# Attention and a gated FFN in one kernel: the first batch's loads laid out and queued anew

## The chip, the cores and the metric

One core of a Trainium2 chip. The metric is device microseconds of one execution. A profile of one execution comes with it; its times are counted from the start of the profiled span.

## The reference

Inputs q, k, v are (batch 8, heads 8, sequence 576, head width 64) in float32. The FFN has model width 512 and inner width 1536.

```python
kv  = einsum('bhsd,bhse->bhde', k, v)
out = einsum('bhsd,bhde->bhse', q, kv)
out = out / sqrt(mean(out*out, -1) + 1e-6) * g_norm
x   = out.transpose(0, 2, 1, 3).reshape(4608, 512)
xn  = x / sqrt(mean(x*x, -1) + 1e-6) * rms_g
y   = (silu(xn @ w_gate) * (xn @ w_val)) @ w_out
```

There is no softmax, so k and v are first reduced to one 64x64 matrix per head, and q is multiplied with that. A sum over tokens may be taken in any grouping of them, provided that k and v are grouped alike.

## The kernel before

The 576 tokens of a batch are cut into 512 "main" tokens and 64 of "remainder". The main tokens lie on 128 partitions with four consecutive tokens each (`NC = 4` chunks), the remainder on 64 partitions with one token each, as a fifth chunk whose other 64 partitions hold zeros. Heads go in four pairs (`j` from 0 to 3), two heads side by side in one 128x128 matmul; `P0` is pairs 0 and 1, `P1` pairs 2 and 3. `H0` and `H1` are the first and last four heads. After the attention of a batch its 512 main tokens go through the FFN, the remainders of all eight batches together at the end. Matmuls are in bf16.

The order of instructions on each engine is written by hand (later batches by a planner with fixed costs, `Placer`). Only the first batch (`Att(0)`) matters here, and of it the first half, chunks 0 and 1 of q, on which the FFN's first matmuls depend:

- Loads: v by POOL's queue with a cast to bf16 on the way (remainder, `H0`, `H1`), straight to `vc[0]`. k by SP's queue as float32 (`H0`, remainder, `H1`). q's chunks 0 and 1 by ACT's queue, then the gains (`grow`, three small loads). q's chunks 2 and 3 are issued on SP and ACT by a wait that is added by hand, once `v_loads[0]`, v's remainder, has landed. The weights follow v on POOL's queue.
- PE: 18 idle matmuls (`spin`, L232), the transposes of q (`qT_mm`, L298), a transpose of the gains (L798), four more idle matmuls, then the kv products of `P0` (`kv_pairs`, L279), o for the statistics (`oT_mm`, L368), the kv products of `P1`, and so on through the statistics (L393), o (L340), the transposes of x (L509) to the first gate matmuls (L662). An engine runs its instructions in the order in which they stand.
- DVE: the memsets at the start (L158 to L169; `idle` among them, which the first spin reads), casts of q's half, of k's `H0` and of k's remainder, the copy of qT of `P1`, the gains, then the masked copies of kv (L286).
- ACT: the copy of qT of `P0` (L320), the cast of k's `H1` (L203), the squares (L379).
- POOL, behind the weights' loads: memsets, and the casts of q's rest (L203, L210).

`kv_pairs` and `pair` take every chunk of a pair:

```python
for c in self.kv_chunks:                 # NC + 1 of them
    nc.tensor.matmul(ps[:, i, :], lhsT=self.pair(1, c, j), rhs=self.pair(2, c, j), ...)
```

Of the kernel before, what the change touches and what calls it, by code (L numbers as in the profile page):

```python
# [10 lines left out]
FP32 = mybir.dt.float32  # L11
BF16 = mybir.dt.bfloat16
# [74 lines left out]
def kernel(  # L87
# [12 lines left out]
    nc = tc.nc  # L100
    B, H, S, D = q.shape
# [3 lines left out]
    NC = 4  # L105
    MAIN = 128 * NC
    REM = S - MAIN
# [9 lines left out]
    pool = lambda name, bufs, **kw: ctx.enter_context(tc.tile_pool(name=name, bufs=bufs, **kw))  # L117
    consts = pool("consts", 1)
    stage = pool("stage", 3)
    rstage = pool("rstage", 4)  # L120
    qkv = pool("qkv", 2)
    outa_p = pool("outa", 6)
    sq_p = pool("sq", 3)
# [17 lines left out]
    vc, kc = ([consts.tile([128, H, (NC + 1) * D], BF16, name=f"{t}c{n}") for n in range(2)] for t in "vk")  # L141
    sel = consts.tile([128, 2, 2], BF16, name="sel")
    qc = consts.tile([128, H, (NC + 1) * D], BF16, name="qc1")
# [8 lines left out]
    wo = [consts.tile([128, OB, d_model], BF16, name=f"wo{n}") for n in range(NF // OB)]  # L152
    kvs = [consts.tile([128, NS, 2, D], BF16, name=f"kvs{n}") for n in range(2)]
    qTs = [consts.tile([128, NC + 1, NS, 128], BF16, name=f"qTs{n}") for n in range(2)]
    rems = [[consts.tile([128, H, D], BF16, name=f"rem{t}{n}") for n in range(m)] for t, m in (("q", 2), ("k", 1))]
    xr = consts.tile([128, NS, MAIN], BF16, name="xr")
    for t in range(2):
        nc.vector.memset(rems[t][0][REM:], 0.0)  # L158
    nc.vector.memset(vc[0][REM:, :, NC * D :], 0.0)
    idle = consts.tile([128, MAIN], BF16, name="idle")  # L160
    nc.vector.memset(idle, 0.0)  # L161
    nc.vector.memset(diag, 0.0)
# [9 lines left out]
    src = (q, k, v)  # L172
# [3 lines left out]
    def load_main(b, t, heads=(0, H), cs=(0, NC), queue=nc.sync):  # L176
        if (b, t) not in staged:
            staged[b, t] = stage.tile([128, H, NC * D], FP32, name="stg")
        h0, h1 = heads
        view = src[t][b, :, 0:MAIN, :].rearrange("h (p c) d -> p h (c d)", c=NC)  # L180
        return queue.dma_start(
            out=staged[b, t][:, h0:h1, cs[0] * D : cs[1] * D], in_=view[:, h0:h1, cs[0] * D : cs[1] * D]
        )

    def load_cast(b, t, heads=None):
        to = qc if t == 0 else (vc if t == 2 else kc)[b % 2]
        if heads is None:
            return nc.gpsimd.dma_start(
                out=to[:REM, :, NC * D :], in_=src[t][b, :, MAIN:S, :].rearrange("h p d -> p h d")
            )  # L190
        view = src[t][b, :, 0:MAIN, :].rearrange("h (p c) d -> p h (c d)", c=NC)[:, heads[0] : heads[1]]
        return nc.gpsimd.dma_start(out=to[:, heads[0] : heads[1], : NC * D], in_=view)

    def load_rem(b, t, queue=nc.sync):
        rstaged[b, t] = rstage.tile([REM, H, D], FP32, name="rstg")
        return queue.dma_start(out=rstaged[b, t], in_=src[t][b, :, MAIN:S, :].rearrange("h p d -> p h d"))

    def cast_main(b, t, eng, heads=(0, H), cs=(0, NC)):
        if (b, t) not in mains:
            mains[b, t] = qkv.tile([128, NC, H, D], BF16, name=f"main_{'qkv'[t]}")  # L200
        h0, h1 = heads
        copy = eng.copy if eng is nc.scalar else eng.tensor_copy
        return copy(  # L203
            out=mains[b, t][:, cs[0] : cs[1], h0:h1, :],
            in_=staged[b, t].rearrange("p h (c d) -> p c h d", c=NC)[:, cs[0] : cs[1], h0:h1, :],
        )

    def cast_rem(b, t, eng):
        copy = eng.copy if eng is nc.scalar else eng.tensor_copy
        copy(out=rems[t][b % 2][:REM], in_=rstaged[b, t])  # L210
# [6 lines left out]
    def loads_kv(b):  # L217
        return [lambda t=t, hs=hs: load_cast(b, t, hs) for t in (1, 2) for hs in ((0, H), None)]
# [11 lines left out]
    def spin(ps, n):  # L230
        for _ in range(n):
            nc.tensor.matmul(ps, lhsT=idle[:, :128], rhs=idle, start=True, stop=True, skip_group_check=True)  # L232

    def flat(ps):
        return ps.rearrange("p j t -> p (j t)")

    class Att:
# [35 lines left out]
        def kv_pairs(self, js, wait=0):  # L273
            ps = mm1_p.tile([128, 4, 2 * D], FP32, name="mm1")
            spin(flat(ps), wait)
            ps = ps[:, : len(js)]
            for i, j in enumerate(js):
                for c in self.kv_chunks:
                    nc.tensor.matmul(  # L279
                        ps[:, i, :], lhsT=self.pair(1, c, j), rhs=self.pair(2, c, j),  # L280
                        start=i == 0 and c == 0, stop=i == len(js) - 1 and c == NC, skip_group_check=True,
                    )
            return ps

# [472 lines left out]
    V, G, A = nc.vector, nc.gpsimd, nc.scalar  # L757
    H0, H1 = (0, 4), (4, 8)
    P0, P1 = (0, 1), (2, 3)
    ALL = range(NS)  # L760
    v_loads = [load_cast(0, 2, hsx) for hsx in (None, H0, H1)]
    load_main(0, 1, H0)
    load_main(0, 0, cs=(0, 2), queue=A)
    load_rem(0, 1)
    load_main(0, 1, H1)
    A.preload_act_table(ACT.Sqrt)
    A.dma_start(out=grow[0:NS], in_=moe_rms_g.rearrange("(s p) -> s p", p=128))
    for half in range(2):
# [9 lines left out]
    w_loads = [load_w(n) for n in range(len(FB))]  # L778
    G.memset(rems[0][1][REM:], 0.0)
    G.memset(kvs[1], 0.0)  # L780
    for tile_ in (kc[0], kc[1], vc[1], qc):
        G.memset(tile_[REM:, :, NC * D :], 0.0)

    def fold(w, s, eng):
        if eng == "ACT":
            A.mul(out=w[:, s], in_=w[:, s], mul=gain[:, s : s + 1])  # L786
        else:
            V.tensor_scalar(out=w[:, s], in0=w[:, s], scalar1=gain[:, s : s + 1], scalar2=None, op0=OP.mult)

    spin(mm1_p.tile([128, MAIN], FP32, name="mm1"), 18)  # L790
    a = Att(0)
    cast_main(0, 0, V, cs=(0, 2))
    cast_main(0, 1, V, H0)
    cast_rem(0, 1, V)
    for js, eng in ((P0, A), (P1, V)):
        a.qT_out(a.qT_mm(js, (0, 1)), js, 0, eng)
    gT = o2_p.tile([128, NS + 1], FP32, name="o2")
# [3 lines left out]
    for half in range(2):  # L801
        rows = slice(half * D, (half + 1) * D)
        V.tensor_tensor(out=sel[rows, 1, half : half + 1], in0=gcol[rows], in1=gcol[rows], op=OP.mult)
    V.tensor_scalar(
        out=gain, in0=gall[:, 0:NS], scalar1=gcol, scalar2=float(d_model) ** 0.5, op0=OP.mult, op1=OP.mult
    )
    kva = a.kv_pairs(P0, 4)
    cast_main(0, 1, A, H1)
    for i, j in enumerate(P0):
        a.kv_pairs_out(kva, i, j)  # L810
    ta = a.oT_mm(P0, 0, 2, o2_p, 2)
# [23 lines left out]
    for t in (0, 2, 1):  # L835
        load_cast(1, t, (0, H))
        load_cast(1, t)
# [6 lines left out]
    for n, w in enumerate(FB):  # L844
        js = range(FB0[n], FB0[n] + w)
# [68 lines left out]
    for b in range(1, B):  # L914
# [9 lines left out]
        if b == 1:  # L924
            for n, at in ((0, 6), (1, 24), (2, 30), (3, 40)):
                for j in range(NS):
                    for w, eng, cost in ((wg, "DVE", 0.09), (wv, "ACT", 0.13)):
                        f = P.put(eng, cost * FB[n], lambda w=w, n=n, j=j, e=eng: fold(w[n], j, e), at=starts[1] + at + j)
# [36 lines left out]
```

## Time and profile before

| | us |
|---|---|
| median of 3 runs | 329.57 (329.0 to 476.69) |
| the profiled execution, its own time | 329.4 |
| its span | 327.6 |
| PE busy | 318.6 (97% of the span) |
| DVE, ACT, POOL busy | 176.0, 144.5, 89.0 |
| PE busy in 0 to 10 / 10 to 20 / 20 to 40 us | 7.50 / 7.52 / 20.00 |
| first kv product (L279) | 11.44 |
| first gate matmul (L662) | 18.55 |

The execution takes 1.8 us more than its span, for what lies before the first and after the last instruction. Busy time on PE counts the idle matmuls too. In the timelines a row gives start, duration, engine, source line, operation, output and inputs, count, and in brackets how long the engine had been idle and what ended that.

### The profile page before, as it was taken

What the parts mean: (1) busy time and instruction counts of PE and PEld (TensorE: products, weight loads), DVE (VectorE), ACT (ScalarE), POOL (GpSimd) and SP (SyncE); (2) the same over time, 40 slices, a digit from 0 to 9 for tenths busy, and PEclk for the clock granted to TensorE, in tenths of its full rate; (3) what the DMA queues carried; (4) which work ended last, traced back from release to release, by engine and by line L of the source; (5) the groups of instructions that cost most, each with busy time, mean ns of one, the idle gap of its engine ahead of it and who ended that gap; (6) DMA issues with size and microseconds to landing.
All of it is one profiled execution on the core that took longest, in us unless ns stands there. A gap on an engine that the chain in (4) does not pass through costs nothing.

```text
span 327.6 us, 5425 instructions
## 1 busy us (share of the span) xinstructions
PE 318.6 (97%) x2060; PEld 162.2 (49%) x2060; DVE 176.0 (54%) x392; ACT 144.5 (44%) x269; POOL 89.0 (27%) x109
## 2 busy tenths in 40 slices
PE   7789999999999999999999999999999999999995
PEld 2468765554445444544454445444544444444443
DVE  3458446679928681768077807781687234203411
ACT  1375446776658422842274227421752233223320
POOL 8663320028205800580058004900420000000000
PEclk9999999999999999999999999999999999999999
DMA  8999999774994895589557966696000800020013
GB/s 193 227 200 199 194 223 212 179 175 53 167 208 136 103 157 161 145 98 140 161 167 84 136 166 176 70 148 168 35 1 0 170 32 0 13 116 2 0 34 96
DMA packets 78741, 40.49 MB, mean 124 GB/s; under 512 B 42744, under 2 KB 74236, under 8 KB 78716
## 3 DMA queue, kind: packets, MB, share of 16 engines
q0 software_dynamic: 30928, 14.16, 34.2%
q1 hardware_dynamic: 46048, 25.08, 31.9%
q10 hardware_dynamic: 1740, 0.92, 1.0%
q8 instruction: 16, 0.26, 0.3%
q14 instruction: 9, 0.07, 0.1%
HBM read 37.78 MB, written 9.44 MB: 144 GB/s over the span
## 4 chain that ended last, share of the span: by engine, by line
PE 94%; DMA 3%; DVE 1%; issue 0%; POOL 0%; ACT 0%; DVEq 0%; POOLq 0%
PE mm L634 57%; PE o L669 26%; DMA vc<-in_v_dram 3%; PE att L331 2%; PE att L268 2%; PE mm L669 2%; PE o L698 1%; PE att L309 1%; PE o L368 0%; DVE xna L350 0%; PE att L509 0%; PE mm L279 0%; PE att L368 0%; PE mm L662 0%; PE mm L232 0%
## 5 line engine op out<-in xcount | busy, mean ns | idle before, releaser
L652 DVE TENSOR_TENSOR h<-silu,mm 128x512 bf16<-128x512 bf16 (+1 forms) x120 | 75.7, 632 | 79.6 <-PE mm L634 69.3
L643 ACT ACTIVATE silu<-mm 128x512 bf16<-128x512 f32 (+1 forms) x120 | 66.4, 556 | 89.1 <-PE mm L634 80.2
L634 PE MATMUL mm<-x,wv 128*128 128x512 bf16 (+1 forms) x432 | 99.8, 355 | 0.0
L634 PE MATMUL mm<-x,wg 128*128 128x512 bf16 (+1 forms) x420 | 98.7, 358 | 0.0
L669 PE MATMUL o<-wo,h 128*128 128x512 bf16 x396 | 89.9, 379 | 0.0
L414 POOL TENSOR_TENSOR sq<-sq,g 128x512 bf16<-128x512 bf16 x30 | 34.4, 1153 | 134.2 <-ACT sq L357 134.2
L634 PEld LDWEIGHTS <-wg 128*128 128x128 bf16 x468 | 45.0, 98 | 45.9
L634 PEld LDWEIGHTS <-wv 128*128 128x128 bf16 x480 | 45.4, 98 | 40.9
L669 PEld LDWEIGHTS <-h 128*128 128x128 bf16 x420 | 40.3, 98 | 46.9
L685 ACT COPY osb<-o 128x512 f32<-128x512 f32 x33 | 19.3, 589 | 67.8 <-PE o L669 67.8
L419 DVE TENSOR_REDUCE st<-sq 128x8 f32<-128x512 bf16 x60 | 38.4, 679 | 0.0
L292 DVE CAST kvs<-att 64x256 bf16<-64x256 f32 x14 | 5.9, 422 | 39.5 <-PE att L268 39.4
L483 DVE TENSOR_TENSOR xna<-outa,al 128x512 bf16<-128x512 bf16 x35 | 21.8, 686 | 0.0
L357 ACT ACTIVATE sq<-att 128x512 bf16<-128x512 f32 x30 | 18.2, 607 | 0.0
L361 ACT CAST outa<-att 128x512 bf16<-128x512 f32 x30 | 17.8, 594 | 0.0
L331 PEld LDWEIGHTS <-qTs 128*128 128x128 bf16 x140 | 9.8, 98 | 5.2
L634 PE MATMUL mm<-xr,wg 128*128 128x512 bf16 x48 | 12.3, 379 | 0.0
L634 PE MATMUL mm<-xr,wv 128*128 128x512 bf16 x48 | 12.3, 379 | 0.0
L331 PE MATMUL att<-kvs,qTs 128*128 128x128 bf16 x140 | 11.7, 219 | 0.0
L203 POOL CAST main_q<-stg 128x1024 bf16<-128x1024 f32 (+1 forms) x12 | 11.4, 987 | 0.1
L232 PE MATMUL mm<-idle 128*128 128x512 bf16 x27 | 8.0, 455 | 2.1 <-DVE idle L161 2.1
L786 ACT ACTIVATE wv<-wv,gain 128x384 bf16<-128x384 bf16 x16 | 9.2, 612 | 0.2 <-PE mm L634 0.2
(130 smaller groups left out, 175.4 us busy)
## 6 DMA issues: line engine op xcount, KB each, us to landing
out_dram<-osb SPq DMA_DIRECT2D x32, 256.0 KB, 2.3
stg<-in_q_dram SPq DMA_DIRECT2D x6, 1024.0 KB, 6.8
vc<-in_v_dram POOLq DMA_DIRECT2D x7, 512.0 KB, 8.4
kc<-in_k_dram POOLq DMA_DIRECT2D x7, 512.0 KB, 6.2
wg<-in_moe_w_gate_dram POOLq DMA_DIRECT2D x4, 384.0 KB, 16.1
wv<-in_moe_w_val_dram POOLq DMA_DIRECT2D x4, 384.0 KB, 17.1
wo<-in_moe_w_out_dram POOLq DMA_DIRECT2D x4, 384.0 KB, 13.6
stg<-in_k_dram SPq DMA_DIRECT2D x2, 512.0 KB, 7.1
```

Of the source, the lines that this page charges most:

```text
L203: return copy(out=mains[b, t][:, cs[0] : cs[1], h0:h1, :], in_=staged[b, t].rearrange("p h (c d) -> p c h d", c=NC)[:, cs[0] : cs[1], h0:h ...
L331: nc.tensor.matmul(o[:, 2 * j : 2 * j + 2, :], lhsT=self.qTj[:, j, c, :], rhs=self.kv[:, j, :, :], start=j == 0, stop=j == NS - 1, skip_gr ...
L357: nc.scalar.activation(out=self.sq[c][:, 0], in_=self.o[c], func=ACT.Square)
L361: (eng.tensor_copy if eng else nc.scalar.copy)(out=self.outa[c], in_=self.o[c])
L414: eng.tensor_tensor(out=self.sq[c][:, 1], in0=self.sq[c][:, 0], in1=g2, op=OP.mult)
L419: nc.vector.reduce_sum(out=self.st[:, which, c, :], in_=self.sq[c][:, which], axis=AX.X)
L483: return eng.tensor_tensor(out=self.xna[:, c], in0=src, in1=self.al[:, c, :].to_broadcast([128, H, D]), op=OP.mult)
L634: nc.tensor.matmul(ps[:, : c1 - c0], lhsT=w[n][:, s, jj * 128 : (jj + 1) * 128], rhs=x_of(g, s, c0, c1), start=s == 0, stop=s == NS - 1)
L643: nc.scalar.activation(out=sis[g, j][:, c0:c1], in_=ps, func=ACT.Silu)
L652: nc.vector.tensor_tensor(out=hs[g, j][:, c0:c1], in0=sis[g, j][:, c0:c1], in1=v_ps, op=OP.mult)
L669: nc.tensor.matmul(ps, lhsT=hs[g, j][:, t * 128 : (t + 1) * 128], rhs=wo[j // OB][:, j % OB, :], start=j == 0, stop=j == NF - 1)
L685: (eng.copy if eng is nc.scalar else eng.tensor_copy)(out=o, in_=ps)
```

## The change

- v's and k's remainders of the first batch are laid out as 32 partitions of two consecutive tokens each: `vr` and `krT`, new tiles. A packet of the load is then 512 B and not 256 B, and there are 256 of them and not 512.
- The kv sum of the first batch has six chunks: four main and two of remainder. Each pair has six matmuls.
- The two new tiles are cleared below row 32 by four DVE memsets; the old ones for k's remainder and `vc[0]` go. `vc[0]`, which a later batch still uses, is cleared on POOL.
- k's `H0` stays on SP's queue, k's `H1` goes from SP's to ACT's as its first load, q's half goes from ACT's to SP's behind k's `H0`. k's remainder goes from SP's to ACT's queue, behind k's `H1`, into a buffer of the pool `stage`; the pool `rstage` has two buffers and not four.
- On DVE the cast of k's `H0` stands before that of q's half, and the cast of k's remainder (32x1024) after it. On ACT the cast of k's `H1` stands before the copy of qT. In the program as built, ACT's third gains load waits until k's `H1` has landed.

```diff
-    rstage = pool("rstage", 4)
+    rstage = pool("rstage", 2)
...
-    rems = [[... name=f"rem{t}{n}") for n in range(m)] for t, m in (("q", 2), ("k", 1))]
+    rems = [[consts.tile([128, H, D], BF16, name=f"remq{n}") for n in range(2)]]
+    krT = consts.tile([128, 2, H, D], BF16, name="remk")
+    vr = consts.tile([128, H, 2, D], BF16, name="remv")
...
-    for t in range(2):
-        nc.vector.memset(rems[t][0][REM:], 0.0)
-    nc.vector.memset(vc[0][REM:, :, NC * D :], 0.0)
+    for tile_, rows in ((krT, REM // 2), (vr, REM // 2), (rems[0][0], REM)):
+        for r0 in (rows, 2 * rows) if rows < REM else (rows,):
+            nc.vector.memset(tile_[r0 : REM if r0 < REM else 128], 0.0)
...
+    def two(t):
+        return src[t][0, :, MAIN:S, :].rearrange("h (p c) d -> p h (c d)", c=2)
...
-                for c in self.kv_chunks:
+                for c in range(NC + 2):
+                    h = slice(2 * j, 2 * j + 2)
+                    if c < NC:
+                        k_, v_ = self.pair(1, c, j), self.pair(2, c, j)
+                    else:
+                        k_, v_ = krT[:, c - NC, h, :], vr[:, h, c - NC, :]
...
-    v_loads = [load_cast(0, 2, hsx) for hsx in (None, H0, H1)]
+    v_loads = [G.dma_start(out=vr[: REM // 2].rearrange("p h c d -> p h (c d)"), in_=two(2))]
+    v_loads += [load_cast(0, 2, hsx) for hsx in (H0, H1)]
     load_main(0, 1, H0)
-    load_main(0, 0, cs=(0, 2), queue=A)
-    load_rem(0, 1)
-    load_main(0, 1, H1)
+    load_main(0, 1, H1, queue=A)
+    load_main(0, 0, cs=(0, 2))
+    krst = stage.tile([128, H, NC * D], FP32, name="stg")[: REM // 2, :, : 2 * D]
+    A.dma_start(out=krst, in_=two(1))
...
-    for tile_ in (kc[0], kc[1], vc[1], qc):
+    for tile_ in (kc[0], kc[1], vc[0], vc[1], qc):
...
+    cast_main(0, 1, V, H0)
+    cast_main(0, 1, A, H1)
     cast_main(0, 0, V, cs=(0, 2))
-    cast_main(0, 1, V, H0)
-    cast_rem(0, 1, V)
+    V.tensor_copy(out=krT[: REM // 2], in_=krst.rearrange("p h (c d) -> p c h d", c=2))
...
     kva = a.kv_pairs(P0, 4)
-    cast_main(0, 1, A, H1)
```

More of the change, by code (lines that the diff above doesn't have):

```diff
@@ L154 @@
     qTs = [consts.tile([128, NC + 1, NS, 128], BF16, name=f"qTs{n}") for n in range(2)]
-    rems = [[consts.tile([128, H, D], BF16, name=f"rem{t}{n}") for n in range(m)] for t, m in (("q", 2), ("k", 1))]
+    rems = [[consts.tile([128, H, D], BF16, name=f"remq{n}") for n in range(2)]]
+    krT = consts.tile([128, 2, H, D], BF16, name="remk")
+    vr = consts.tile([128, H, 2, D], BF16, name="remv")
     xr = consts.tile([128, NS, MAIN], BF16, name="xr")
-    for t in range(2):
-        nc.vector.memset(rems[t][0][REM:], 0.0)
-    nc.vector.memset(vc[0][REM:, :, NC * D :], 0.0)
+    for tile_, rows in ((krT, REM // 2), (vr, REM // 2), (rems[0][0], REM)):
+        for r0 in (rows, 2 * rows) if rows < REM else (rows,):
+            nc.vector.memset(tile_[r0 : REM if r0 < REM else 128], 0.0)
     idle = consts.tile([128, MAIN], BF16, name="idle")
@@ L277, in kv_pairs @@
             for i, j in enumerate(js):
-                for c in self.kv_chunks:
+                for c in range(NC + 2):
[4 more added lines that the diff above has]
+                        k_, v_ = krT[:, c - NC, h, :], vr[:, h, c - NC, :]
                     nc.tensor.matmul(
-                        ps[:, i, :], lhsT=self.pair(1, c, j), rhs=self.pair(2, c, j),
-                        start=i == 0 and c == 0, stop=i == len(js) - 1 and c == NC, skip_group_check=True,
+                        ps[:, i, :], lhsT=k_, rhs=v_,
+                        start=i == 0 and c == 0, stop=i == len(js) - 1 and c == NC + 1, skip_group_check=True,
                     )
```

## The prediction

> **What bounds the kernel now.** I read the page first. The chain that ended last is PE work almost throughout, with one DMA left on it.
>
> ```profile
> PE 94%; DMA 3%; DVE 1%; issue 0%; POOL 0%; ACT 0%; DVEq 0%; POOLq 0%
> ```
>
> From about 18.5 us on PE runs without a hole worth naming, so the end moves only if the start of that stream moves. What sets the start is in the chain in order of time, cut to the first 20 us (start, us, what):
>
> ```profile
> 1.26 0.86 POOL vc L188
> 2.12 9.27 DMA vc<-in_v_dram
> 11.40 0.04 issue
> 11.44 0.72 PE mm L279 x10
> ```
>
> The first kv products (L279) wait for the first half of v, landed at 11.40. From there to 18.55 everything is a chain of short steps, each waiting for the last. So I ask when that L279 can start after the change. The timelines of PE and DVE say what stands ahead of it on its engine (start, us, instruction, and in brackets the idle time before it):
>
> ```profile
> 7.32 0.69 DVE L203 CAST main_q<-stg 128x1024 bf16<-128x1024 f32 x1 [4.44 <-DMA stg<-in_q_dram]
> ...
> 8.07 0.62 PE L298 MATMUL att<-ident,main_q 128*128 128x128 bf16 x8 [0.19 <-DVE main_q L203]
> 8.62 0.22 PE L798 MATMUL o<-identf,grow 5*128 5x5 f32 x1
> 8.77 1.04 PE L232 MATMUL mm<-idle 128*128 128x512 bf16 x4
> 11.44 0.38 PE L279 MATMUL mm<-vc,main_k 128*128 128x128 bf16 x4 [1.63 <-DMA vc<-in_v_dram]
> ```
>
> PE works in order: the transposes of q (L298), the transpose of the gains (L798) and four idle matmuls stand ahead of L279. q landed just under 7.32, and L279 could have started at 8.77 + 4 x 0.216 = 9.64, which is 2.35 us after q landed (0.03 to the cast, 0.69 cast, 0.06, then 1.57 from 8.07 to 9.64). Now that is hidden behind v. It stops being hidden when q lands later than 11.44 - 2.35 = 9.1.
>
> The third view is the DMA packets by queue in short windows. q0 is POOL's queue, q1 SP's, q10 ACT's; the columns are packets, MB and share. q0's MB are bf16 as written; the reads are twice that. First the window 0 to 5 us, then 5 to 10, then 12.5 to 13:
>
> ```profile
> q1 hardware_dynamic: 520, 0.52, 33.0%
> q10 hardware_dynamic: 591, 0.30, 20.4%
> ...
> q1 hardware_dynamic: 1046, 0.65, 60.3%
> q0 software_dynamic: 1040, 0.32, 58.2%
> q10 hardware_dynamic: 461, 0.22, 16.2%
> ...
> q0 software_dynamic: 68, 0.05, 66.3%
> q1 hardware_dynamic: 67, 0.03, 33.5%
> q10 hardware_dynamic: 68, 0.03, 22.9%
> ```
>
> By 5 us SP's half of k is through (512 packets) and ACT's half of q (1024 packets of 512 B) more than half. From 5 to 10 the engines read 0.65 + 0.64 + 0.22 = 1.51 MB, 0.30 MB/us, and are never idle. The last three rows are the key: three queues with packets of different sizes move the same number of packets, so queues share by packets, not by bytes. A transfer cut into small packets loses against one in large packets.
>
> **The change, part by part.** The program's lists of instructions and waits show what moves.
>
> q's first half goes from ACT's queue, where it was first, to SP's queue behind k's first half. Work left when SP gets to it, at 5.0: k's second half now runs where q ran, and by 5.0 has moved between 0.30 MB (q's bytes) and 0.45 (q's packet count, mostly, at 1 KB), so 0.07 to 0.22 are left; k's remainder 0.13; q 0.52. On POOL's queue: q has 1024 packets, and in as many turns POOL moves v's remainder (256), v's first half (512) and 256 of its second half: 0.13 + 0.52 + 0.26. In all 1.63 to 1.78 MB; at 0.30 to 0.33 MB/us (the 5-to-10 rate, and 0.30 + 0.03 MB in the row of 4.5 to 5.5 below) 4.9 to 5.9 us, so q's packets end at 9.9 to 10.9. In before q's packets were through at about 6.3 and it landed just under 7.32, 1.0 later: so 10.9 to 11.9. If bytes were shared alike, POOL would move 0.52 in that time and not 0.91, and q would land 1.2 us sooner, 9.7 at the bottom. I take 11.1, in the lower part of the band by packets, since the equal counts speak for it and the remainders' packets cost less (next). L279 then starts at 11.1 + 2.35 = 13.45 in place of 11.44: **+2.0 us**.
>
> k and v remainders: 256 packets of 512 B each in place of 512 of 256 B. The windows 4.5 to 5.5 and 5.5 to 7 us show both sizes, ACT's q at 512 B and then the two remainders:
>
> ```profile
> q10 hardware_dynamic: 599, 0.30, 102.5%
> q1 hardware_dynamic: 41, 0.03, 10.2%
> ...
> q1 hardware_dynamic: 550, 0.20, 70.8%
> q0 software_dynamic: 508, 0.06, 65.8%
> q10 hardware_dynamic: 145, 0.06, 17.7%
> ```
>
> In the second, 1203 packets, nearly all of 256 B, took 1.5 us, 1.25 ns each over the 16 engines; in the first, 599 of 512 B took 1 us, 1.67 ns each. Both remainders: 1024 x 1.25 = 1.28 us of all engines before, 512 x 1.67 = 0.86 after, a gain of 0.4, counted already in my 11.1. v's first half should land nearer 10.7 than 11.40, which no longer decides. POOL's issue for v's remainder (0.87 now, 0.69 for the same shape later) falls or stays: 0 to -0.3, hidden behind the same wait.
>
> Six chunks in place of five: one more L279 for each of four pairs, 0.056 each by their pitch (ten from 11.44 to 11.99), all on the path: 4 x 0.056 = **+0.2**.
>
> DVE memsets: three of 64x256 at 0.27 become one of these and four of 512 elements. 512 elements are not in the trace on DVE; 0.27 is the floor, and twice 0.27 (the 64x256 and 128x256 forms cost the same, so elements count) the ceiling. I take the ceiling: PE's idle matmuls start at 3.6 instead of 2.11 and end at about 9.2 instead of 7.7. Nothing is due before q's cast at 11.1: zero, and without that cover +1.5 on L298.
>
> k's remainder cast: 32x1024, strided like main_k's 0.88, instead of 0.42, and now between q's cast and DVE's copy of qT. DVE then is done with qT, gall, sel and gain at q + 0.72 + 0.88 + 0.41 + 0.71 = q + 2.7, ahead of the kv products' end at q + 3.0: zero. k's second half is cast by ACT at 8 to 9 instead of 11.24; its reader is the second group of L279, so also zero.
>
> Waits: ACT's second grow load now waits for k's second half, and behind it stand ACT's load of q's rest, the cast of k's second half and the copy of qT. L798 on PE needs that grow load. By the queue it can land at about 10; L798 is not due before 11.1 + 0.78 + 0.55 = 12.4. Zero here, a rival below. POOL has one memset more (0.52) before the casts of q's rest; their reader L298 at 20.24 had 2.3 us to spare after 17.93.
>
> Sum: 2.0 + 0.2 = +2.2 on the profiled execution's 329.4 (span 327.6 and 1.8 around it): **331.6 us**. The median of the runs shown is 329.57, the same within 0.2. For q's landing between 9.7 and 11.9 the sum gives 330.2 to 332.4.
>
> **Rivals.**
>
> (1) q is in time, and the kernel is no slower. If SP's queue moves q before v gets its turns (ACT's queue alone did 599 packets in 4.5 to 5.5), q lands at 9.1 or sooner. Then two things decide: the later idle matmuls, 9.2 + 0.05 + 1.57 = 10.8, and v's first half at 10.2 to 10.7. L279 starts at 10.2 to 10.9: -0.5 to -1.2, plus 0.2: 328.4 to 329.1, say 328.9. Against it are the equal packet counts; for it, that POOL's packets came only at 5.4 us. It decides below a landing of 9.1.
>
> (2) The grow load. Issued when k's second half lands, at some 7.3, as q's half did, it may be slow: the 32 KB gbc load took 4.8 us to land and q's rest on ACT's queue 8.3, so it lands at 12.1 to 15.6. At 12.1 it costs nothing; at 15.6 L279 starts at 15.6 + 0.15 + 0.86 = 16.6, for 334.8. In before, the same loads had landed by 8.62, behind a whole half of q, and PE did not wait for them. At 13.5 the time is 332.7. It decides from 12.4 on.
>
> (3) PE's clock. PE would sit idle from 9.2 to 11.9, 2.7 us; before, 1.63 us changed nothing (L279 kept 0.056). At the start the first eight idle matmuls took 3.59 us, the later four 1.04 us, though PEclk shows full speed. If the pause brings back the slow pitch, 8 transposes (+0.45), 4 idle ones (+0.84), 12 kv products (+0.67) double: 331.6 + 1.9 = 333.5.
> The Trainium skill (TensorE: Matmul & The Clock Gate, Part 1: The HAM clock gate) says that the clock halves after an idle window of about 3.4 us, free-running; by it a pause of 2.7 us is safe and one past 3.4 (q at 11.8 or later) is not.
>
> (4) The start slips and later slack takes it up (PE is 9.72 of 10 us busy in 40 to 50): 329.6. Little speaks for it; PE is full from 20 to 40.
>
> **How the numbers follow.** Forecast 0.55, rival 1 0.22, rival 2 0.10, rival 3 0.08, rival 4 0.05. The forecast's own range is 330.2 to 332.4. The whole range takes in most of rival 1 and rival 3: 328.8 to 333.4. A measurement of this kernel tells about 2% from no change, 6.6 us; every case lies inside. Past it on the slow side needs the late grow load and the cold clock together and more (0.04); on the fast side nothing reaches (0.01).
>
> **What would show it.** Right: DVE's cast of main_q starts after 10.4 with a wait on DMA stg<-in_q_dram, L298 follows, L279 starts near 13.5 with no idle time on v, the chain's first DMA is q's. Wrong: main_q cast before 9.1 and L279 at 11 or sooner with a wait on vc (rival 1); L798 with idle time of its own (rival 2); idle matmuls behind L298 at 0.43 each (rival 3); a first L662 about 2 us later with the span unchanged (rival 4).

## The result and the profile after

The changed kernel takes 330.91 us (median of 5 runs, 330.55 to 331.48) against 329.31 for the kernel before in the same session: 1.6 us more, ratio 1.0046, 95% interval 1.0035 to 1.0057. That is slower, by less than 2%. One of the five runs of before took 476.69 us; such a run is left out of the ratios. A second set of runs gave 330.64 against 329.19, 1.0042 (1.0030 to 1.0054). The profiled execution has a span of 328.8 us.

The chain in order of time, cut to the first 21 us (start, us, what), has another DMA at its head and then only PE and one cast:

```profile
1.26 8.72 DMA stg<-in_q_dram
9.99 0.02 issue
10.01 0.70 DVE main_q L208
10.71 0.05 issue
10.76 0.62 PE att L308 x8
11.38 0.15 PE o L811
11.54 0.97 PE mm L237 x4
12.50 0.67 PE mm L289 x12
```

Before, the DMA there was v's first half, and L279 followed its landing by 0.04 us. Now it is q's half, and between its landing and the kv products (now L289) stand the cast, the transposes and the four idle matmuls that used to be hidden. The timeline of PE shows the start of L289 and that nothing but q holds it:

```profile
3.98 5.58 PE L237 MATMUL mm<-idle 128*128 128x512 bf16 x18 [3.98 <-DVE idle L163]
10.76 0.62 PE L308 MATMUL att<-ident,main_q 128*128 128x128 bf16 x8 [1.20 <-DVE main_q L208]
11.31 0.22 PE L811 MATMUL o<-identf,grow 5*128 5x5 f32 x1
11.47 1.04 PE L237 MATMUL mm<-idle 128*128 128x512 bf16 x4
12.34 0.39 PE L289 MATMUL mm<-vc,main_k 128*128 128x128 bf16 x4
```

L289 starts at 12.34, without idle time of its own: v's first half had landed at 10.27, 1.1 us sooner than in the first profile of before, and k's second half at 6.21, 5 us sooner. Neither helps, because PE has not reached the instruction that reads them. From 12.34 on the steps are those of before, with the sixth chunk in each kv product; the first gate matmul starts at 19.68 (18.55 before), and PE is full after it.

### The profile page after: what moved, and what is told of

Same layout as the page of the kernel before. It is cut to its first block, busy times and chain, and to the rows that moved or that the text cites. A ratio compares the mean times of both kernels' runs of the same rounds, so it can differ in the third digit from the quotient of the medians.

```text
span 328.8 us, 5438 instructions
## 1 busy us (share of the span) xinstructions
PE 318.4 (97%) x2064; PEld 162.4 (49%) x2064; DVE 177.7 (54%) x394; ACT 144.3 (44%) x269; POOL 89.3 (27%) x110
## 4 chain that ended last, share of the span: by engine, by line
PE 95%; DMA 3%; DVE 1%; issue 0%; ACT 0%; SPq 0%; DVEq 0%
PE mm L644 57%; PE o L679 26%; DMA stg<-in_q_dram 3%; PE att L341 2%; PE att L273 2%; PE mm L679 2%; PE mm L237 1%; PE o L708 1%; PE att L319 1%; PE att L519 1%; PE o L378 0%; PE mm L289 0%; PE att L308 0%; PE att L378 0%; PE mm L672 0%; PE att L350 0%
```

## The experiments

All are compared with the kernel before on the same chip. "First kv" is the start of the first kv product, "first gate" that of the first gate matmul, both from the run's profile.

| run | first kv, us | first gate, us | span, us | ratio to before (95%) |
|---|---|---|---|---|
| before, first profile | 11.44 | 18.55 | 327.6 | |
| before, second profile | 10.77 | 17.88 | 327.3 | |
| changed | 12.34 | 19.68 | 328.8 | 1.0046 (1.0035 to 1.0057) |
| changed, again | 12.19 | 19.53 | 329.0 | 1.0042 (1.0030 to 1.0054) |
| layout alone | 11.95 | 19.28 | 328.5 | 1.0013 (1.0003 to 1.0023) |
| queues alone | 11.85 | 18.97 | 328.0 | 1.0018 (1.0009 to 1.0027) |
| changed, kv ahead of q on PE | 11.29 | 19.11 | 328.3 | 1.0015 (1.0006 to 1.0023) |
| changed, idle memset first | 12.61 | 19.95 | 329.3 | 1.0078 (1.0056 to 1.0099) |
| the same, 30 idle matmuls | 12.51 | 19.84 | 329.3 | 1.0047 (1.0033 to 1.0060) |
| the same, 14 idle matmuls | 13.52 | 21.50 | 330.8 | 1.0101 (1.0085 to 1.0116) |
| layout alone, idle memset first | 10.45 | 17.78 | 327.3 | 1.0000 (0.9991 to 1.0009) |
| kv ahead of q, idle memset first | 10.26 | 18.08 | 327.2 | 1.0009 (0.9998 to 1.0020) |
| layout, idle first, v's half first | 9.75 | 17.63 | 327.7 | 1.0009 (1.0000 to 1.0018) |
| the same, q's rest freed | 9.86 | 17.63 | 327.2 | 0.9987 (0.9978 to 0.9996) |

**The kernel before, profiled again.** No edit.

> The kernel before, unchanged, profiled a second time. In its first profile each load's last two of sixteen shares of a landing came 0.4 to 0.8 us after the others (v's first half 11.40, the fourteenth share 10.63); in the changed kernel's all sixteen came within 0.2 to 0.4 us. If that is a trait of the one execution, v's first half lands near 10.7 here, L279 starts near 10.8 and the span is some 0.6 us shorter than 327.6. If it is a trait of the kernel (its 256-byte packets, or v's remainder on 64 partitions), L279 starts at 11.4 again.

The late shares are a trait of the execution. v's first half landed at 10.73 (its fourteenth share at 10.48) and L279 started at 10.77; the span fell by only 0.3 us. So the first profile of before, on which the prediction rests, shows L279 some 0.7 us later than it need be. Something else differed too: the 18 idle matmuls took 6.87 us and not 5.76.

```profile
2.11 6.87 PE L232 MATMUL mm<-idle 128*128 128x512 bf16 x18 [2.11 <-DVE idle L161]
8.82 0.61 PE L298 MATMUL att<-ident,main_q 128*128 128x128 bf16 x8
```

In that row L298 has no idle time: PE, not q's cast (done at 7.46), held it. The slow pitch at the start lasted for 13 matmuls here and for 8 in the first profile.

**The layout alone.** The 32-partition remainders, six chunks and memsets of the change, with before's queues and order of casts (the lines of the casts are left out here):

```diff
     load_main(0, 1, H0)
-    load_main(0, 1, H1, queue=A)
-    load_main(0, 0, cs=(0, 2))
+    load_main(0, 0, cs=(0, 2), queue=A)
     krst = ...
-    A.dma_start(out=krst, in_=two(1))
+    nc.sync.dma_start(out=krst, in_=two(1))
+    load_main(0, 1, H1)
```

> The 32-partition remainders, six chunks and their memsets stay; the queues and the order of the casts are those of before (q first on ACT's queue, k's remainder and second half on SP's). Theory (q's landing behind k's first half on SP costs the time): q lands near 7 us again and does not decide; L289 starts at the later of v's first half (10.3 to 10.9) and the idle matmuls' end at 9.4 + 1.57 = 11.0, so 11.0; with six chunks 0.2 more than before's chain: ratio to before 0.998 to 1.001. Rival (the layout itself costs: memsets, six chunks, the strided cast of k's remainder): L289 at 12 or later and a ratio of 1.003 to 1.005 as in the full change.

Between the two theories: 1.0013. q landed at 7.27 and v's first half at 10.40, but L289 started at 11.95, because PE's idle matmuls, which start only at 3.99 behind the new memsets, kept PE until 10.38:

```profile
10.38 0.61 PE L308 MATMUL att<-ident,main_q 128*128 128x128 bf16 x8
10.92 0.22 PE L810 MATMUL o<-identf,grow 5*128 5x5 f32 x1
11.07 1.04 PE L237 MATMUL mm<-idle 128*128 128x512 bf16 x4
11.95 0.39 PE L289 MATMUL mm<-vc,main_k 128*128 128x128 bf16 x4
```

So the late start of the idle matmuls can cost, once q is in time. A part of it here is the slow pitch, which lasted for 12 of them. The run of this layout with the memset of idle first, below, is free of the penalty.

**The queues alone.** before with k's second half first on ACT's queue, q's half behind k's first on SP's, k's remainder on ACT's, and the casts in the changed order; remainders on 64 partitions.

> The queues and the order of the casts are those of the changed kernel; the remainders stay on 64 partitions in 256-byte packets, with five chunks and the old memsets. Theory: q lands at 10.0 to 10.6 (10.0 in the changed kernel; 512 packets more stand in the queues), L279 starts 2.35 us later, at 12.35 to 12.95, and the ratio is 1.003 to 1.005 although PE has four matmuls fewer and its idle matmuls start 1.9 us sooner. Rival (layout): q's place costs nothing, L279 at 11.4 to 11.6 and a ratio of 0.999 to 1.001.

q landed at 9.50, sooner than I gave it, L279 started at 11.85 = 9.50 + 2.35, with DVE's q cast as the releaser of L298:

```profile
10.27 0.62 PE L298 MATMUL att<-ident,main_q 128*128 128x128 bf16 x8 [1.97 <-DVE main_q L203]
```

The mechanism stands, the ratio is 1.0018 and not 1.003: without the layout the queues cost less than half of the 1.0046. The two parts do not simply add up, 1.0013 and 1.0018 against 1.0046. One reason lies in q's landing: in the seven traces with the new layout and q behind k on SP's queue q landed at 9.71 to 10.26, 9.98 in the mean, against 9.50 in this one trace. An estimate from these numbers: 0.6 us for the queues alone, 0.5 for q's later landing and 0.2 for the sixth chunks make 1.3 of the 1.45 to 1.6 us. That the smaller packets are why q lands sooner here is likely, but no run separates it.

**kv ahead of q on PE.** The changed kernel in another order:

```diff
+    V.tensor_copy(out=krT[: REM // 2], ...)
     cast_main(0, 0, V, cs=(0, 2))
-    V.tensor_copy(out=krT[: REM // 2], ...)
+    kva = a.kv_pairs(P0, 4)
+    for i, j in enumerate(P0):
+        a.kv_pairs_out(kva, i, j)
     for js, eng in ((P0, A), (P1, V)):
         a.qT_out(a.qT_mm(js, (0, 1)), js, 0, eng)
```

> The changed kernel with one difference of order: on PE the kv products of the first two pairs stand ahead of the transposes of q, on DVE the cast of k's remainder ahead of that of q and the masked copies of kv ahead of the copy of qT. Theory (q is late, and what it costs is that kv stands behind it on PE): L289 starts when v's first half lands, 10.3 to 10.5; the transposes follow at 11.0, the first L378 at 12.1 to 12.3 (13.56 in the changed kernel, 12.54 before); ratio to before 0.998 to 1.000. Rival (the grow load or DVE decides): L378 at 13 or later, ratio 1.002 to 1.005.

It takes back most of the loss (1.0015), less than the theory had it: L289 started at 11.29 and the first L378 (o for the statistics) at 13.09, as late as the rival gave it, but neither the grow load nor DVE held it, since PE has no idle time between the two. v's first half was there at 10.01; the idle matmuls, 22 in a row from 3.99 on, held PE until 11.29.

**The idle memset first,** on the changed kernel:

```diff
+    idle = consts.tile([128, MAIN], BF16, name="idle")
+    nc.vector.memset(idle, 0.0)
     for tile_, rows in ((krT, REM // 2), ...):
```

> The changed kernel with the memset of idle moved ahead of the other memsets on DVE, so that PE's 18 idle matmuls start near 1.3 us and not at 3.98, and end by 8 however long the slow pitch lasts (7 to 13 of them at 0.427 in the six traces so far). Theory (q's landing decides): L308 follows q's cast as before, q lands at 9.5 to 10.0, L289 at 11.9 to 12.4, ratio 1.003 to 1.005, no better than the changed kernel in this call by more than 0.2 us. Rival (the late memset costs much of it): L289 at 11.5 or sooner, ratio 1.001 or less.

Both theories missed: 1.0078, clearly slower than the changed kernel. L308 still waits for q's cast, so the memset was indeed hidden. But PE now stands still for 3.40 us:

```profile
1.20 6.43 PE L237 MATMUL mm<-idle 128*128 128x512 bf16 x18 [1.20 <-DVE idle L160]
11.03 0.62 PE L308 MATMUL att<-ident,main_q 128*128 128x128 bf16 x8 [3.40 <-DVE main_q L208]
```

In this profiled execution (331.1 us) L308 keeps its 0.62 for eight. The clock that was granted to PE, which is on record for every run as a mean over the span, splits this kernel's six runs: the two at 1.0 took 330.5 and 331.1 us, about the changed kernel's own time, the four at 0.989 to 0.995 took 331.9 to 333.4. The next two runs ask whether the pause is the cause.

> The changed kernel with the memset of idle first (as in the run that came out at 1.0078) and 30 idle matmuls at the start in place of 18, so that PE is busy until 9.1 to 10.4 and the pause ahead of L308 is under 1.7 us. Theory (what made that run slower was the pause of up to 3.4 us and the slow pitch after it, not q): ratio 1.003 to 1.0055, like the changed kernel, with L289 at 12.0 to 12.6. Rival (the earlier memset harms something else): ratio 1.006 or more again.

> The same with 14 idle matmuls at the start: PE then idles from 5.8 to 7.1 on, 4 us or more ahead of L308. Theory (a pause of that length brings the slow pitch back): the trace shows L308 at 0.11 each and the idle matmuls behind it at 0.43, L289 at 13.3 to 13.6, and the ratio is 1.008 to 1.013. Rival (the pitch does not fall back in a pause): L308 at 0.056 each and a ratio of 1.003 to 1.006.

With 30 idle matmuls the pause is gone, the ratio is 1.0047, and the mean granted clock is 0.998 to 1.0 in all five runs. With 14 the pause is 4.57 us, the ratio 1.0101, and the mean granted clock 0.988 to 0.995 in all four. The timeline of the latter, and its window from 10 to 12 us (the window's length, busy time of PE, weight loads, DVE, ACT and POOL, then the granted clock, DMA's share and GB/s):

```profile
10.68 1.03 PE L308 MATMUL att<-ident,main_q 128*128 128x128 bf16 x8 [4.57 <-DVE main_q L208]
11.84 1.89 PE L237 MATMUL mm<-idle 128*128 128x512 bf16 x4
13.52 0.63 PE L289 MATMUL mm<-vc,main_k 128*128 128x128 bf16 x4
...
10.00:12.00 2.00, 1.32 (x10) 1.08 (x11) 1.46 (x3) 0.90 (x2) 0.98 (x2) 0.50 1.39 201
```

The clock is at 0.50; the four idle matmuls take 1.89 us and not 1.04, and L289 starts 2.84 us after L308 and not 1.58. The pause of 4.57 us brought the slow clock back. From L308 to the first gate matmul it is 10.82 us here and 8.92 with the pause of 3.40 us, so it costs 1.9 us. The pause of 3.40 us did not bring it back in the one traced execution. In that kernel's four longer runs the mean granted clock fell as it does with 14 idle matmuls, so the slow clock came back in them too; where, and after how long a pause, is not traced. The Trainium skill (TensorE: Matmul & The Clock Gate, Part 1: The HAM clock gate) puts the fall at an idle window of about 3.4 us, free-running; both traces agree with it, the clock staying up after 3.40 us and at 0.50 after 4.57.

**The layout alone with the idle memset first,** and **kv ahead of q with it:**

> The layout alone (queues and casts as before) with the memset of idle first. In the run without that, PE's idle matmuls ran from 3.99 to 10.38 and L289 started at 11.95 although v's first half had landed at 10.40. Theory (the four longer memsets cost by the idle matmuls when q is early): L289 starts when v's first half lands, 10.3 to 10.5, the first L378 at 11.6 to 11.8, ratio 0.996 to 0.999. Rival (the six chunks and the strided cast cost it): L289 at 11 or later, ratio 1.000 to 1.002.

> The changed kernel with kv's products ahead of q's transposes on PE, and the memset of idle first. In the run without that, the 22 idle matmuls from 3.99 on kept L289 until 11.29, with v's first half landed at 10.01. Theory: L289 starts with v's first half at 10.0 to 10.4, the first L378 at 11.8 to 12.1, ratio 0.996 to 0.999. Rival (the second grow load, landed at 10.7, or DVE's order decides): L378 at 12.5 or later, ratio 1.000 to 1.002.

Both lose the whole penalty, 1.0000 and 1.0009, the latter's interval taking in no change, but neither shows the gain that was expected. The 1.0009 comes from three of twelve runs, 330.4 to 330.6 us at a mean granted clock of 0.994 to 0.995; the nine others, at 0.998 to 1.0, have a mean of 329.15 us, against 329.21 for before. The starts were right, 10.45 and 10.26, each within 0.05 of v's first half:

```profile
10.45 0.38 PE L289 MATMUL mm<-vc,main_k 128*128 128x128 bf16 x4 [0.69 <-DMA vc<-in_v_dram]
```

That is the row of the layout with the memset first. Its first gate comes 0.77 us sooner than in the first profile of before, its span is only 0.3 us shorter. The second profile of before shows the same. Each of the two meets a wait that the first profile of before does not have, ahead of the gate matmuls at 28.8: 0.3 us for DVE (L360) in the layout's run, 0.2 for the weights wg in the second profile of before. An earlier start is partly given back. The rest of that 0.5 us is not traced to a cause.

**v's first half ahead of v's remainder,** and then **q's rest issued on k's remainder:**

```diff
-    v_loads = [...vr..., H0, H1]
+    v_loads = [H0, ...vr..., H1]
...
-        tc.add_manual_dep(rest.ins, v_loads[0].ins.name, SYNC, ...)
+        tc.add_manual_dep(rest.ins, kr_load.ins.name, SYNC, ...)
```

Both stand on the layout alone with the memset of idle first. The first has only the first part of this edit; there the wait for `v_loads[0]` means v's first half.

> The layout with the queues of before and the memset of idle first (ratio 1.000), and v's first half ahead of v's remainder on POOL's queue. L289 then waited for v's first half at 10.40; its packets now start 1 us sooner. Theory (v's first half alone held L289): it lands at 9.3 to 9.8, the remainder at 9.6 to 10.0 (six chunks into L289's sum), L289 starts at 9.8 to 10.0, ratio 0.997 to 0.9995. Rival (k's second half or v's second half becomes late instead, for the same bytes have to land): the second group of L289 waits, ratio 1.000 to 1.002.

> As the run with v's first half ahead of its remainder (ratio 1.0009: L289 at 9.75, but L308 for q's remainder then idle for 0.9 us behind POOL's cast of it, since q's rest was issued only when v's first half had landed, 9.71); here q's rest is issued when k's remainder has landed, about 7.4. Theory (an early start is given back where q's remainder comes late): that wait is gone, span 326.6 to 327.1, ratio 0.998 to 0.9995. Rival (q's rest takes turns from v and k, or the weights come later): L289 at 10.5 or later, or a wait for wg of 0.5 us or more, ratio 1.000 to 1.002.

In the first, L289 started at 9.75, but the ratio is 1.0009. v's remainder landed at 10.35, later than expected, and held the fifth chunk for 0.26 us; and then q's rest, issued at 9.72 and not at 8.38 as in the layout's run, came late (PE's waits):

```profile
PE att L308 <- POOL remq L215: 0.9, 1, 0.9
```

With q's rest freed that wait is gone and the ratio is 0.9987 (0.9978 to 0.9996): the only version that is faster than the kernel before, by 0.4 us.

## Why the prediction held, and where it was off

**What bounds the start, and the 2.35 us.** Right. q landed at 9.99, L289 started at 12.34, exactly 2.35 later; 9.50 and 11.85 in the run of the queues alone. v does not decide.

**q's landing.** The step that was off: 11.1 forecast, 9.99 measured (9.83 in the second profile), near the bottom of my bounds at 9.7. There are two errors, counted from the middle of my band, 10.4 for the end of q's packets and 11.4 for the landing. The first, 0.9 us, is POOL's share. The packets between 5 and 9.5 us, and the half microsecond from 6.5:

```profile
q0 software_dynamic: 739, 0.30, 52.6%
q1 hardware_dynamic: 1045, 0.53, 51.4%
q10 hardware_dynamic: 455, 0.29, 21.2%
...
q0 software_dynamic: 98, 0.03, 49.0%
q1 hardware_dynamic: 98, 0.05, 49.0%
q10 hardware_dynamic: 100, 0.05, 33.8%
```

In that half microsecond the three queues moved 98, 98 and 100 packets, each of 512 B as read. But POOL moved 739 packets while q moved its 1024, not as many, since v's first packets came only at 5.8 us: in the half microsecond from 5.5 SP's queue moved 236 and POOL's 18. From 6 to 9.5 the two were near each other, 757 and 721. 285 packets of 1 KB are 0.29 MB, 0.9 us at the 0.32 MB/us of this window; the middle of my band for the end of q's packets, 10.4, less 0.9 is 9.5, where they did end. The second, 0.5 us, is the time from the last packets to the landing: 1.0 taken, 0.5 measured. The 1.0 came from an execution in which two of the sixteen shares of each load were 0.5 to 0.85 us late (q's 0.7); in the second profile of before q's were 0.1 late.

The prediction's rule that queues share by packets is too strong. It roughly fits the changed kernel from 6 us on, but from 6 to 7.5 in the profile of before, which the prediction does not show, SP's queue moved 600 packets and POOL's 293, although both had loads that were issued and had not landed. From 6.5 to 7 in the run of the queues alone SP's moved 159 packets of 512 B, POOL's and ACT's 100 and 87 of 256 B as read. What sets the shares in such windows the runs do not show.

**Six chunks, +0.2.** Right: in the chain the L289 blocks are 0.67 for twelve, and the second L279 block 0.56 for ten; from their first product to the idle matmul behind it the first blocks take 0.67 (12.34 to 13.01) and 0.55 (11.44 to 11.99). From first kv to first gate the changed kernel takes 7.34 us and before 7.11.

**The memsets at nothing.** Right in the changed kernel, where q's cast ends at 10.70 and PE's idle matmuls at 9.6 (10.2 in the second profile). But the cover is thin, 0.4 to 1.2 us, and my 9.2 for their end left out that the slow pitch lasts differently from execution to execution. They start at 3.98 (forecast 3.6): each of the four memsets of 512 elements took 0.49, inside my ceiling of twice 0.27, but with what lies between them they took 2.38 us, from 0.91 to 3.29. Without the cover they do cost: in the layout alone L308 starts at 10.38, with idle first at 8.01, and L289 at 11.95 against 10.45. Not all of this is the memsets'. The idle matmuls started 2.8 us later, but their slow pitch also lasted for 12 matmuls and not 6, some 1.3 us at 0.427 against 0.216 each, and with idle first it is q's cast that holds L308. By the runs the difference of the two versions is 0.0013, some 0.4 us.

**k's remainder cast, the grow load, POOL's memset at nothing.** Right. The cast took 0.68. The gains load that waits for k's second half was issued at 6.23 and landed at 10.67, 0.64 us ahead of L811; rival 2 did not come about.

**The rivals.** Rival 1 (q in time) failed by 0.9 us of q's landing. Its mechanism was there, SP's queue moving q while POOL's had hardly begun, but for half a microsecond only (236 packets against 18). Rival 3, the clock, did not decide here: the pause ahead of L308 was 1.20 us and 0.42, and the ten runs of the changed kernel have a mean granted clock of 0.998 to 1.0. It is real, at 4.57 us. Its price was forecast at 1.9 and came to 1.9. It also explains why removing the hidden memset alone made things worse: the late idle matmuls were what kept PE busy until shortly before q. Rival 4, later slack, did not come about: between the two first profiles the first gate moved by 1.13 us and the span by 1.2.

**The sum.** +2.2 forecast, +1.6 and +1.45 measured. In the two first profiles L289 is +0.90 and the chunks +0.22, together 1.12 of the span's 1.2; against the second profile of before, whose v was not late, the first gate is +1.8 and the span +1.5. The sign, the place and the chain were right; the late landing in the profile of before hid a part of the loss, 0.7 us by L279's start and 0.3 by the span, and the forecast had q 1.1 us too late. These two errors go against each other, so that the forecast came within 0.6 to 0.75 us of the measured loss is in part luck.

## What to carry to other kernels

A load that was hidden has a due time given by what stands behind its reader on an in-order engine, not by its own reader: q was not needed before kv in the data flow, but kv stood behind q's transposes on PE. Before moving a load behind another one, work out when it lands by counting packets in all queues, with the time at which each queue's first packet moves (POOL's only at 5.8 us here), and compare that with the slack of the first instruction queued behind its consumer. And where idle matmuls bridge a wait, treat start, length and pause as one thing: taking delay out of their start can lengthen the pause past the point at which the clock falls.

## What the runs showed of the hardware that was not expected

- The slow pitch at the start lasted for 2.5 to 6.0 us of busy PE over the fourteen traces, 6 to 14 idle matmuls at 0.427 us, and differed between executions of one kernel (3.4 and 5.5 us in before). The Trainium skill (TensorE: Matmul & The Clock Gate, Part 1: The HAM clock gate) gives about 3.4 us of sustained work with half a microsecond either way, and adds that the number of slow matmuls differs between runs of one kernel. Here the time varied by more than the half microsecond. The granted clock column shows 1.00 during that start, and 0.50 only after the later pause.
- The last of sixteen shares of each early load came 0.5 to 0.85 us behind the fourteenth in one execution of before and at most 0.4 in the other. One profile cannot tell a landing time better than that.
